# Attention and feed-forward kernel ordered by a planner: planned durations set anew, and the order rules of its stages chosen again

## The chip, the cores and the metric

The kernel runs on one core of a Trainium2 chip. The metric is the device time of one execution in microseconds; the median of several runs counts. The engines are called TensorE (PE), VectorE (DVE), ScalarE (ACT), GpSimd (POOL) and SyncE (SP).

## The reference

```python
x = A_x                                   # (1, 2048, 640) bf16
xn = _layernorm(x, axis=-1)
# A: 32 query heads of 20, one key and one value head for all of them
q = (xn @ wq).reshape(B, S, 32, 20).transpose(0, 2, 1, 3)
k = xn @ wk;  v = xn @ wv                 # (1, 2048, 20) each
p = softmax(einsum("bhqd,bkd->bhqk", q, k) * 20 ** -0.5)
a = einsum("bhqk,bkd->bhqd", p, v).transpose(0, 2, 1, 3).reshape(B, S, 640) @ wo
# B: 640 -> 1536 -> 640
h = relu(xn @ w1 + b1);  f = (h * h) @ w2 + b2
return x + a + f
```

## The kernel before

The work of attention is cut into 32 blocks: 4 chunks of 512 queries by 8 groups of 4 heads. A block has 16 key tiles of 128 keys, and each of them 4 score tiles (one per head) of 128 keys by 512 queries, so there are 2048 score tiles. TensorE makes a score tile into one PSUM bank; the four heads of a group lie on four row groups of the array, so that up to four score tiles run at once in one "visit" (the code's mode "R"). All other matmuls run in mode "C", four at once on four column groups. The planner charges `SWITCH` for a change of mode.

A score tile gets its exponential in one of two ways:

- ScalarE takes two neighbouring PSUM banks in one ACTIVATE (`make_act`, L1008; seldom one or three) and writes to the ring PT. When the four heads of a key tile are there, one group of four matmuls (`PV...`) adds its share of the values to the block's accumulator in PSUM.
- A *set* is a key tile whose four heads go to VectorE (`make_dqk`, `after_dqk`). VectorE makes a 16-bit integer from the score (L1197, `D1_...`), which read as bf16 is a straight-line approximation of a power of two. Three further terms are made from it by adding constants: *passes* `P1` to `P3`, on GpSimd (`int64_add`, four 16-bit elements at a time, L1217) or on VectorE (L1219). Each of the four terms would be a group of four value matmuls (`DPV...`). Two terms can be added up beforehand, which saves one group: by a DMA that accumulates and is issued from GpSimd (`AD...`, L1232) or by VectorE. The term buffers lie in the tensor tmore and, from the tenth on, in x_sb, which is no longer used by then.

Between them run the rest: layer norm at the start, the projections, the feed-forward part (`FFN...`, L738, L746), the output products, the normalisation of a block (`emit_norm`, through DRAM), and the tail with the last 512 rows.

The order of every engine's instructions is found when the kernel is built, by a list scheduler with planned durations: each `Op` has an engine, a duration and dependencies, and `ready()` adds a latency for each pair of engines (`LATS`) or one of its own. At each step the candidate that can start earliest is committed, with ties within `EPS` broken by priority. The chip then runs each engine's list in that order, with semaphores for the dependencies; the planned times themselves are not kept. For the adding transfers the planner knows the GpSimd time of an issue (`ADDUR`), the delay when the issue waits for a GpSimd pass (`ADPL`), the way to the start and to the landing (`ADLEAD`, `ADLAND`) and the distance between two transfers (`ADGAP`):

```python
if op.add:
    begun = max(s + ADLEAD, dma_free[0])
    dma_free[0] = begun + ADGAP
    op.lat = begun + ADLAND - op.fin
```

What the scheduler prefers is set by some thirty parameters with `DEFAULTS`; `RULES` overrides them for stages of 10 us (`STG`) of planned ScalarE time, stage 1 to 66 (`next_stage`, `par`). Those that the text below speaks of:

- `ADDM`: how many adding transfers a new set gets on average (0 to 2; `new_set`).
- `KEEP`, `KEEPX`, `KEEPM`: how many free PSUM banks must be left over before a VectorE score tile rides along, starts a visit of its own, or before another matmul unit starts; -1 in KEEPX or KEEPM means KEEP (`pool_banks`).
- `NOPEN`, `DVL`: how many sets may be open, and above what backlog of VectorE no tile is given to it.
- `PBIAS`: a pass goes to VectorE when GpSimd's backlog exceeds VectorE's by more than this many us.
- `MRG`, `M1`: whether two score steps share one visit. `P2`: VectorE tiles in a visit that follows a full one.
- `JIT`: how long before ScalarE runs dry a score step is issued.

GpSimd loads another instruction library (`LIB`) after its part of the layer norm and before its first pass.

## Time and profile before

| | |
|---|---|
| median of 3 runs (lowest to highest) | 670.59 us (669.18 to 670.64) |
| profiled execution, its own time | 671.5 us |
| its span, first to last instruction | 669.7 us |
| granted TensorE clock | 1.00 |
| busy PE, DVE, ACT, POOL | 661.3, 604.2, 651.9, 580.7 us |
| ScalarE's exponentials, VectorE's score tiles | 697, 652 |
| GpSimd's passes, VectorE's passes | 437, 52 |
| adding transfers | 133 |

In a row of the groups, the number behind the bar is busy time in us, then the mean duration of one in ns, then the idle time of the engine just before such instructions and what ended it. In a row of the timeline the first number is the start from the span's begin and the second the length, both in us; "x4" says how many instructions are merged. Durations of one engine can overlap: the next instruction starts before the last has ended. A row of a table by windows has start and end, the length, and then the busy time of PE, PEld, DVE, ACT and POOL, the granted clock, the share of the DMA engines and GB/s.

### The profile page before, as it was taken

The page shows a single profiled execution, that of the slowest core. Times are in us where ns is not written, and L with a number is a line of the kernel's source. Part 1 is how long each engine was busy: PE and PEld are TensorE (multiplying, and loading weights), DVE is VectorE, ACT ScalarE, POOL GpSimd, SP SyncE. Part 2 cuts the span into 40 slices and gives each one's busy share as a digit, 9 for nine tenths or more (in the row PEclk, how much of TensorE's full clock was granted, in tenths as well). Part 3 has the DMA queues.
Part 4 walks back from the last instruction along what each step waited for, and adds up shares of the span by engine and source line. Part 5 has one row for each costly group of instructions (what it writes and reads, how often), then busy time and mean ns, then how long its engine had stood idle before and what let it go on. Part 6 is the DMA issues. An engine that isn't in the chain of part 4 may idle for free.

```text
span 669.7 us, 22479 instructions
## 1 busy us (share of the span) xinstructions
PE 661.3 (99%) x9591; PEld 212.2 (32%) x9592; DVE 604.2 (90%) x1074; ACT 651.9 (97%) x720; POOL 580.7 (87%) x595
## 2 busy tenths in 40 slices
PE   9999999999999999999999999999999999999998
PEld 4532222333322222333333222233333332222354
DVE  8979999999999999998989999998998999999824
ACT  7999999999999999999999999999999999999995
POOL 1729899999999998999999999899999899989901
PEclk9999999999999999999999999999999999999999
DMA  8897776888777877697886876766678876987751
GB/s 289 229 249 158 166 158 131 174 165 170 168 153 140 168 137 135 135 195 156 159 176 121 167 147 123 148 124 140 127 165 167 170 151 131 173 164 150 162 128 52
DMA packets 55998, 105.80 MB, mean 158 GB/s; under 512 B 17106, under 2 KB 33250, under 8 KB 55834
## 3 DMA queue, kind: packets, MB, share of 16 engines
q0 software_dynamic: 19808, 72.36, 58.2%
q1 hardware_dynamic: 35514, 31.63, 16.6%
q8 instruction: 75, 1.23, 0.8%
q10 hardware_dynamic: 576, 0.38, 0.2%
q14 instruction: 25, 0.20, 0.1%
HBM read 22.81 MB, written 9.69 MB: 49 GB/s over the span
## 4 chain that ended last, share of the span: by engine, by line
PE 63%; ACT 19%; DMA 7%; POOL 5%; DVE 3%; issue 1%; SPq 1%; POOLq 0%
PE ps L424 62%; ACT PT L1008 19%; POOL x_sb L1217 3%; DMA tmore<-tmore 2%; POOL tmore L1217 2%; DMA x_sb<-tmore 2%; DVE tmore L1197 1%; DMA x_sb<-x_sb 1%; DMA x_sb<-in_A_x_dram 1%; DMA R<-drs 1%; PE ps L619 1%; POOL x_sb L1232 0%; DVE x_sb L1219 0%; SPq L719 0%; DVE big L746 0%
## 5 line engine op out<-in xcount | busy, mean ns | idle before, releaser
L1008 ACT ACTIVATE PT<-ps 128x1024 bf16<-128x1024 f32 x697 | 642.6, 1092 | 5.0 <-PE ps L424 4.6
L1197 DVE TENSOR_SCALAR tmore<-ps 128x512 uint16<-128x512 f32 x652 | 421.7, 683 | 36.5 <-PE ps L424 30.4
L1217 POOL INT64_ADD x_sb<-tmore x219 | 246.9, 1255 | 30.0 <-DVE tmore L1197 19.8
L424 PE MATMUL ps<-qT,kT 20*128 20x512 bf16 x2048 | 268.2, 384 | 1.7 <-ACT PT L1008 1.0
L1217 POOL INT64_ADD tmore<-tmore x218 | 248.5, 1273 | 22.3 <-DVE OR L1076 12.1
L424 PEld LDWEIGHTS ps<-qT,kT 20*128 20x128 bf16 x2048 | 67.4, 91 | 257.4 <-ACT PT L1008 227.4
L424 PE MATMUL ps<-PT,vx 128*32 128x512 bf16 x1396 | 134.2, 387 | 0.0
L424 PE MATMUL ps<-xnT,w_sb 128*32 128x512 bf16 x960 | 77.2, 383 | 0.2 <-DVE hT_tmp L738 0.2
L424 PE MATMUL ps<-w_sb,big 128*32 128x320 bf16 x1536 | 75.4, 301 | 0.0
L1232 POOL DMA_DIRECT2D tmore<-tmore x66 | 70.9, 1082 | 4.2 <-POOL tmore L1217 3.0
L1232 POOL DMA_DIRECT2D x_sb<-tmore x63 | 67.2, 1067 | 4.0 <-POOL x_sb L1217 2.2
L424 PE MATMUL ps<-tmore,vxs 128*32 128x512 bf16 x648 | 58.8, 383 | 0.6 <-POOL tmore L1217 0.6
L424 PE MATMUL ps<-x_sb,vxs 128*32 128x512 bf16 x636 | 57.5, 382 | 0.2 <-DMA x_sb<-x_sb 0.2
L424 PEld LDWEIGHTS ps<-PT,vx 128*32 128x32 bf16 x1396 | 34.2, 93 | 64.5 <-issue 59.9
L424 PE MATMUL ps<-tmore,vx 128*32 128x512 bf16 x468 | 44.5, 382 | 0.7 <-DMA tmore<-tmore 0.6
L424 PEld LDWEIGHTS ps<-w_sb,big 128*32 128x32 bf16 x1536 | 33.6, 96 | 27.3 <-issue 17.2
L738 DVE TENSOR_SCALAR hT_tmp<-ps,b1col 128x512 bf16<-128x512 f32 x48 | 35.6, 742 | 0.9 <-PE ps L424 0.5
L424 PE MATMUL ps<-xnT,wq_sb 128*32 128x512 bf16 (+2 forms) x480 | 33.8, 356 | 0.0
L424 PE MATMUL ps<-x_sb,vx 128*32 128x512 bf16 x324 | 31.8, 382 | 0.6 <-DMA x_sb<-tmore 0.6
L424 PE MATMUL ps<-wo_c,OC 128*32 128x320 bf16 x608 | 31.3, 301 | 0.0
L424 PEld LDWEIGHTS ps<-xnT,w_sb 128*32 128x32 bf16 x960 | 18.0, 94 | 25.9 <-issue 20.5
L826 DVE TENSOR_TENSOR out_sb<-ps,xr 128x320 bf16<-128x320 f32 x24 | 11.6, 484 | 13.2 <-PE ps L424 13.1
(93 smaller groups left out, 328.5 us busy)
## 6 DMA issues: line engine op xcount, KB each, us to landing
tmore<-tmore POOLq DMA_DIRECT2D x66, 512.0 KB, 5.5
x_sb<-tmore POOLq DMA_DIRECT2D x63, 512.0 KB, 5.4
w_sb<-in_B_w_dram SPq DMA_DIRECT2D x8, 480.0 KB, 11.2
big<-OR SPq DMA_DIRECT2D x71, 40.0 KB
big<-drs SPq DMA_DIRECT2D x71, 40.0 KB
xb<-in_A_x_dram SPq DMA_DIRECT2D x1, 2560.0 KB, 11.9
xb<-b2r POOLq DMA_DIRECT2D x1, 2560.0 KB, 20.3
xr<-xb SPq DMA_DIRECT2D x16, 160.0 KB, 4.4
```

The lines of the kernel that those rows point to most:

```text
L424: return lambda e: e.matmul(out_, l, r, start=start, stop=stop, tile_position=tp, skip_group_check=loose)
L619: return [(lambda e, dt=dt: e.transpose(out=psbf(bk)[:, dt * 128:(dt + 1) * 128], in_=xn_sb[:, st, dt:D:DT], identity=ident[:])) for dt in ...
L738: o = Op(f"RL{qc}_{f}", "DVE", 0.66, [lambda e: e.tensor_scalar(out=hT_tmp[:, k % 2, :], in0=ps[:, bk, :], scalar1=b1col[:, f:f + 1], scal ...
L826: o = Op(f"OE{n}", "DVE", 0.40, [lambda e: e.tensor_tensor(out=out_sb[:, slot, cs], in0=ps[:, bk, 0:HW], in1=xrow(st, cs), op=ALU.add)], [ ...
L1008: return Op(f"ACT{st_['j']}", "ACT", ACB + ACM * n, [lambda e: e.activation(out=PT[:, s0:s0 + n, :], in_=ps[:, b0:b0 + (n - 1) * db + 1:db ...
L1197: d1 = op(f"D1_{n}_{i}", "DVE", 0.60, lambda e: e.tensor_scalar(out=L[:, cs].bitcast(U16), in0=ps[:, bank, :], scalar1=XA, scalar2=XB, op0 ...
L1217: fn = lambda e, T=T, j=j: e.int64_add(out=T.bitcast(I64), in0=L.bitcast(I64), in1=TSTEP * j * 0x0001000100010001)
L1232: p = op(f"AD{a}_{n}", "POOL", ADDUR, lambda e, src=src, dst=dst: e.dma_start(dst, src, accum_op=ALU.add), dp + [ad_last.get(k)], dma=adse ...
```

## The change

No instruction is added or taken away in the code. Planned durations and latencies get other values, and the table RULES is replaced by another, for stages 1 to 66; what order comes out, and how many sets, passes and transfers, the planner decides from them.

```diff
-ADDUR = 0.875
-ADPL = 0.31
+ADDUR = 0.6
+ADPL = 0.62
...
-SWITCH = 0.105
-ACB, ACM = 0.0631, 0.4267
+SWITCH = 0.0995
+ACB, ACM = 0.05, 0.4267
...
-LATS = {("PE", "ACT"): 0.225, ("PE", "DVE"): 0.215, ("ACT", "PE"): 0.155, ...
+LATS = {("PE", "ACT"): 0.225, ("PE", "DVE"): 0.22, ("ACT", "PE"): 0.225, ...
...
-        lib_op = op("LIB", "POOL", 10.8, ...
+        lib_op = op("LIB", "POOL", 12.3, ...
...
-            return Op(f"PV{b}_{kt}", "PE", 0.222, parts, deps)
+            return Op(f"PV{b}_{kt}", "PE", 0.226, parts, deps)
...
-            return Op(f"DPV{b}_{kt}_{term}", "PE", 0.2205, parts, deps)
+            return Op(f"DPV{b}_{kt}_{term}", "PE", 0.226, parts, deps)
...
-                    r[0].lat = 0.425
+                    r[0].lat = 0.45
```

The steps of the other four-matmul units (KT, QC, Q1, FFN1 and the fill) go from 0.2205 to 0.224, those of the output products from 0.136 to 0.138. The pair of ScalarE is thereby planned at 0.05 + 2 x 0.4267 = 0.9034 us instead of 0.9165. Some of the rules, for stages 31, 45, 62 and 66:

```diff
-         31: {'PBIAS': 8, 'NOPEN': 3},
+         31: {'EVP': 0.3, 'PBIAS': 8, 'DGAP': 0.8, 'DLAST': 6, 'DRATE': 0.95, 'BEHIND': 0.12, 'IDLE': 0.3, 'EPS': 0.06, 'MRG': 1, 'M1T': 1.2, 'JIT': 0.8, 'PVA': 0.9, 'ND': 2, 'KEEP': 0, 'ADDM': 1.2, 'KEEPM': 2, 'KEEPX': -1, 'DVL': 99},
-         45: {'IDLE': 0.3, 'URG': 4, 'PVA': 0.8, 'PVD': 1.2, 'PP': 4, 'ND': 1, 'ADDM': 0, 'KEEPX': 2},
+         45: {'EVP': 0.3, 'PBIAS': 8, 'MPRIO': 0.3, 'DGAP': 0.8, 'DLAST': 6, 'DRATE': 0.95, 'BEHIND': 0.12, 'EPS': 0.06, 'MRG': 1, 'M1': 2, 'M1T': 1.2, 'ADDN': 0.6, 'ADP': 5, 'JIT': 0.8, 'R3': 9, 'PVA': 0.9, 'D1P': 0.3, 'ND': 2, 'KEEP': 0, 'ADDM': 1.2, 'KEEPM': 2, 'KEEPX': -1, 'DVL': 1.2, 'P2': 2},
-         62: {'EVP': 0.3, 'DGAP': 1.5, 'DRATE': 0.95, ..., 'NOPEN': 3, ..., 'KEEP': 2, 'ADPM': 2.4, 'KEEPM': 1, 'KEEPX': -1, 'DVL': 0.9, 'P2': 2},
+         62: {'EVP': 0.3, 'PBIAS': 8, ..., 'KEEP': 0, 'ADDM': 1.2, 'KEEPM': 2, 'KEEPX': -1, 'DVL': 99},
-         66: {'DGAP': 0.8, 'IDLE': 0.3, 'URG': 4, 'NOPEN': 1, 'MRG': 0, 'ADDN': 0.2, 'R3': 1, 'QKP': 0, 'ND': 1, 'KEEP': 0, 'KEEPM': 0, 'KEEPX': 2, 'DVL': 0.9}}
+         66: {'EVP': 0.3, 'PBIAS': 8, 'MPRIO': 0.5, 'DGAP': 0, 'DLAST': 6, 'DRATE': 0.95, 'BEHIND': 0.05, 'IDLE': 0.3, 'EPS': 0.03, 'MRG': 0, 'M1': 1, 'M1T': 1.2, 'ADDB': 1, 'JIT': 0.8, 'PVA': 0.9, 'SQP': 2, 'ND': 2, 'KEEP': 0, 'ADDM': 1.2, 'KEEPM': 2, 'KEEPX': -1, 'DVL': 99}}
```

The mean of a parameter over the 66 stages (with its default where a stage has no rule), before and after, for the parameters named above:

| | before | after | stages that differ |
|---|---|---|---|
| ADDM | 0.82 | 0.90 | 41 |
| KEEP | 0.82 | 0.55 | 44 |
| KEEPX | 1.98 | 0.79 | 42 |
| KEEPM | 0.58 | 1.06 | 40 |
| PBIAS | 5.5 | 6.0 | 24 |
| NOPEN | 2.2 | 2.2 | 23 |
| JIT | 0.86 | 0.83 | 40 |
| P2 | 0.26 | 0.44 | 27 |

## The prediction

> **What bounds the kernel now.** I read the page first: busy times and the chain that ended last, then the groups of instructions.

> ```profile
> PE 661.3 (99%) x9591; PEld 212.2 (32%) x9592; DVE 604.2 (90%) x1074; ACT 651.9 (97%) x720; POOL 580.7 (87%) x595
> PE 63%; ACT 19%; DMA 7%; POOL 5%; DVE 3%; issue 1%; SPq 1%; POOLq 0%
> L1008 ACT ACTIVATE PT<-ps 128x1024 bf16<-128x1024 f32 x697 | 642.6, 1092 | 5.0 <-PE ps L424 4.6
> L1197 DVE TENSOR_SCALAR tmore<-ps 128x512 uint16<-128x512 f32 x652 | 421.7, 683 | 36.5 <-PE ps L424 30.4
> ```

> ScalarE's exponentials (L1008) take 642.6 us and sat idle only 5.0. The other 652 score tiles go through VectorE (L1197): four to a set, so 163 sets. ScalarE has the other 2048 - 652 = 1396 tiles, two to a step in 697 steps. Second view, ScalarE's timeline: its start, an undisturbed stretch, and its end.

> ```profile
> 12.24 22.54 ACT L1008 ACTIVATE PT<-ps 128x1024 bf16<-128x1024 f32 x24
> 637.37 15.69 ACT L1008 ACTIVATE PT<-ps 128x1024 bf16<-128x1024 f32 x17
> 629.84 30.01 ACT L1008 ACTIVATE PT<-ps 128x1024 bf16<-128x1024 f32 x31
> ```

> The exponentials run from 12.24 to 629.84 + 30.01 = 659.85 us, and 12.24 + 642.6 + 5.0 + a tail of 669.7 - 659.85 = 9.85 make the span of 669.7. In the second row 17 steps take 15.69; less the last one's 1.09, a step starts every 0.91. So ScalarE gives time back only through fewer steps, not through better order: 697 x 0.91 = 634 of the 647.6 us from first to last is its floor, and 13 us at most are waits.

> TensorE is the other bound. Third view, its timeline in a quiet stretch:

> ```profile
> 485.23 0.39 PE L424 MATMUL ps<-qT,kT 20*128 20x512 bf16 x3
> 485.55 0.40 PE L424 MATMUL ps<-PT,vx 128*32 128x512 bf16 x4
> 485.78 0.39 PE L424 MATMUL ps<-x_sb,vxs 128*32 128x512 bf16 x4
> 486.10 0.39 PE L424 MATMUL ps<-qT,kT 20*128 20x512 bf16 x3
> ```

> From start to start: a group of four value matmuls is followed by the next group after 0.23 (485.55 to 485.78); a visit to the scores takes 0.32 to get in (485.78 to 486.10) and 0.32 to get out (485.23 to 485.55), 0.41 more than one group alone. There is no gap to squeeze in these rows; the changed order helps TensorE only with fewer groups or fewer visits. Fourth view, the stretch in which all engines work, and the waits of two of them:

> ```profile
> 45.00:637.00 592.00, 588.24 (x8208) 174.28 (x8200) 552.73 (x916) 588.38 (x641) 562.81 (x567) 1.00 0.77 155
> POOL x_sb L1217 <- DVE tmore L1197: 19.8, 1, 19.8
> POOL tmore L1217 <- DVE OR L1076: 12.1, 1, 12.1
> ```

> In these 592 us (busy PE, PEld, DVE, ACT, POOL) TensorE and ScalarE are idle under 4 us each, at a granted clock of 1.00; VectorE has 39 us left and GpSimd 29. GpSimd's two long waits lie outside: the library load before 45.6 us, and one after its last transfer. So what a new order can use is GpSimd's and VectorE's rest: more sets relieve ScalarE, more transfers that add two term buffers relieve TensorE.

> **GpSimd's transfer issues.** Here the planned numbers change most (0.875 to 0.6, and the delay behind a pass 0.31 to 0.62).

> ```profile
> 299.15 1.03 POOL L1217 INT64_ADD tmore<-tmore  x1
> 300.47 0.88 POOL L1232 DMA_DIRECT2D tmore<-tmore  x1 [0.30 <-POOL tmore L1217]
> 301.08 3.39 POOL L1217 INT64_ADD tmore<-tmore  x3
> 304.08 1.21 POOL L1232 DMA_DIRECT2D tmore<-tmore  x1
> 304.69 2.71 POOL L1217 INT64_ADD x_sb<-tmore  x2
> L1232 POOL DMA_DIRECT2D tmore<-tmore x66 | 70.9, 1082 | 4.2 <-POOL tmore L1217 3.0
> L1232 POOL DMA_DIRECT2D x_sb<-tmore x63 | 67.2, 1067 | 4.0 <-POOL x_sb L1217 2.2
> ```

> An issue lets the next pass start 0.61 after it (304.08 to 304.69); directly behind the pass that it needs there is 0.30 of waiting first (so 0.91). The old plan charged 0.875 and 1.185, the new 0.6 and 1.22. So the new plan is right for an issue with a pass in between, and charges 0.31 too much for a follower. The durations of 1.07 in the last two rows overlap the next instruction, and I do not take them as the price; they are the rival's.

> There are 133 issues (66 and 63 above and four between other buffers). If none follows its pass, the plan frees 133 x 0.275 = 36.6 us of GpSimd; if all do, it books 133 x 0.035 = 4.7 more. I take half: 66 x 0.275 - 67 x 0.035 = 15.8 us.

> **What the planner can buy with 15.8 us.** (1) *More adding transfers.* One replaces a group of four matmuls: 0.23 of TensorE for 0.61 of GpSimd. The share of them per set (ADDM) averages 0.82 over the 66 stages in the old rules and 0.90 in the new: 0.077 x 163 = 12 more. TensorE -12 x 0.23 = -2.8 us, GpSimd +7.3. Their landings are hidden behind other value groups as now. If that cover is gone a landing is paid in full, as at one place of the chain:

> ```profile
> 579.33 9.34 DMA tmore<-tmore
> 589.48 11.14 ACT L1008 ACTIVATE PT<-ps 128x1024 bf16<-128x1024 f32 x12 [0.64 <-PE ps L424]
> ```

> There the landing of 9.34 cost ScalarE 0.64 of idle time. (2) *More sets.* The new rules hold fewer PSUM banks back before a VectorE tile may start (KEEPX averages 1.98 before, 0.79 after; KEEP 0.82 and 0.55) and let GpSimd's backlog grow further (PBIAS 5.5 to 6.0). A set takes two steps off ScalarE, 2 x 0.91 = 1.8 us; on TensorE it takes off two visits (2 x 0.41, if its tiles ride along in other visits) and adds four groups, less the one that it replaces and 0.9 for transfers (2.1 x 0.23): -0.34. It costs VectorE 4 x 421.7/652 = 2.6 and GpSimd three passes of 1.01 and 0.9 x 0.61 = 3.6. What remains of the 15.8 after (1) is 8.5, so two sets: ScalarE -3.6, TensorE -0.7, VectorE +5.2 of its 39, GpSimd +7.2. No row gives the number of sets of the new order; the bounds are three fewer and six more, since six at 3.6 = 21.6 with (1) already take GpSimd's whole 29. Two is my choice within it.

> (3) *The library load*, planned at 10.8, now 12.3:

> ```profile
> 32.64 0.87 POOL L508 TENSOR_SCALAR big<-x_sb,mv,rstd 128x640 bf16<-128x640 bf16 x1
> 45.61 4.08 POOL L1217 INT64_ADD tmore<-tmore  x4 [12.09 <-DVE OR L1076]
> 45.61 2.06 POOL tmore L1217 x2
> 47.71 15.53 PE ps L424 x195
> 48.47 25.97 ACT L1008 ACTIVATE PT<-ps 128x1024 bf16<-128x1024 f32 x28 [0.48 <-PE ps L424]
> ```

> 33.51 to 45.61 is 12.1. The third and fourth rows are pieces of the chain; they show TensorE held by those late passes, and ScalarE lost 0.48. A plan that knows it puts other work there: -0.5 on both (bounds 0 and -0.5).

> (4) *The rest of the numbers.* Value groups go from 0.2205 or 0.222 to 0.226, projections to 0.224, a mode switch from 0.105 to 0.0995, a ScalarE pair from 0.9165 to 0.9034, ScalarE to TensorE from 0.155 to 0.225. Against rows of 0.23, 0.41 and 0.91 these are small, and they charge no time themselves; they alter which instruction the search puts next. A better match should save part of ScalarE's 5.0 us of idle time and of its 13 us over the floor, but a new order can also add waits: between +3 and -5, and I take -1.0, a fifth of the visible idle time.

> Sum on ScalarE's path: -3.6 - 0.5 - 1.0 = -5.1. On TensorE's: -2.8 - 0.7 - 0.5 - 1.0 = -5.0. Neither bound hides the other, so I take the smaller, **-5.0 us**. The start (12.24) and the tail (9.85) stay but for what the rules of the first and last stages shuffle, at most 1 us either way. Against the profiled execution: 671.5 (span 669.7 and 1.8 around it) - 5.0 = 666.5. That execution is 0.9 above the median of 670.59; on the median, **665.6**.

> What moves past what, with the passes that VectorE makes:

> ```profile
> L1219 DVE TENSOR_SCALAR tmore<-tmore 128x2048 uint16<-128x2048 uint16 x27 | 21.0, 786 | 0.2 <-PE ps L424 0.2
> L1219 DVE TENSOR_SCALAR x_sb<-tmore 128x2048 uint16<-128x2048 uint16 x25 | 20.8, 838 | 0.7 <-PE ps L424 0.7
> ```

> The rules set the order of every engine's list, SP's and GpSimd's included. A transfer issue that is put behind a further pass lands 1.01 later, and the group that reads it waits in TensorE's list in order, with the next score visit queued behind it, and ScalarE behind that. With PBIAS raised, some of VectorE's 52 passes go to GpSimd, and each holds what is queued behind it there for 1.01.

> **Rivals.** *A. Larger gain.* If all 36.6 us are freed and go into transfers, that is 60 x 0.23 = 13.8 us of TensorE, and ScalarE would need seven sets to follow, one above the bound. I cap it at -12.6: 658. Against it: ADDM rises by 0.077 only.

> *B. No gain.* That the durations were set to recorded ones would not hold in full: the follower's 0.62 against a recorded 0.30. If the rules still let half of the issues follow, plan and chip have the idle 0.3 as before, no set is added, and the saved library wait is what is left: 670, the same. For it: the charge for a follower hardly changes (1.185 to 1.22). The bound of "same" here is 0.3%, 2 us, about what a measurement of this kernel can tell from no change.

> *C. Slower: GpSimd falls behind its own plan.* The price of an issue on the chip may be more than 0.6, because VectorE's operations hold it up.

> ```profile
> L1232 POOL DMA_DIRECT2D tmore<-tmore x66: 843/1004/1733, 61.9 to 635.7; - x66
> L1232 POOL DMA_DIRECT2D x_sb<-tmore x63: 844/930/1931, 55.9 to 623.5; - x63
> L1217 POOL INT64_ADD x_sb<-tmore x219: 1027/1197/1993, 51.1 to 658.9; - x110
> L1217 POOL INT64_ADD tmore<-tmore x218: 1027/1312/2002, 45.6 to 634.1; - x109
> ```

> Issues reach 1.7 and 1.9 us (minimum, median, maximum in ns). With 145 issues and 219 + 218 + 6 = 443 passes at 1.01, GpSimd's load is 447 + 145c. It fills the 592 us at c = 1.0; the old plan's 0.875 to 1.185 covered that, the new 0.6 does not. At c = 1.07, the mean of the rows, it is 602: 10 us too many. Term buffers then come free late, VectorE waits for them, its PSUM banks are held, and TensorE and ScalarE stop. Half of the 10 us would be taken up by the idle time that GpSimd has; I give +5.4, 676. Against it: the 0.61 from start to start in both examples, which says that much of 1.07 is overlap. [...]

> *D. Slower for lack of cushion.* A planned pair of 0.9034 lies below the 0.91 of the rows; the old 0.9165 lay above, and 697 x 0.013 = 9 us of planned slack vanish. Scores are then placed a little too early and TensorE stands in order before a bank that ScalarE has not left. If a third of the 9 us returns as waits and no set is added: +3, 674.

> **How the numbers follow.** Forecast 0.45 (its own range 661 to 668.5), A 0.11, B 0.14, C 0.22, D 0.08. Faster by over 0.3%: 0.45 + 0.11 = 0.56; within: 0.14; slower: 0.22 + 0.08 = 0.30. The range of 658 to 676 takes in A's and C's prices and leaves out about half of C and of A, under 2 in 10.

> **What would show it.** Right: L1197 at 660 or so instead of 652 and L1008 near 693; some 145 rows of L1232; GpSimd's busy time nearer 592 in the same stretch; no 0.48 of ScalarE before 48 us. Step (1) is wrong if L1232 stays at 133; step (2) if L1197 does not rise. C would show as waits of L1197 for L1217 or for landings, and as ScalarE idle time above 10 us; D as the step count unchanged with more waits. The prediction is wrong altogether if the number of sets falls.

## The result and the profile after

The changed kernel took 698.88 us (median of 6 runs, 693.16 to 709.51) against 670.51 for the kernel before. The ratio is 1.0394, with a 95% interval of 1.0341 to 1.0447; here and below, ratios leave out the runs that lie more than 1.5% above the quickest of the same kernel, in which the clock was lowest. The forecast was 665.6 in a range of 658 to 676. The runs after spread widely, and the mean clock that TensorE was granted goes with their times; the spans and mean granted clocks were 691.4 (0.988) in the quickest and 707.7 (0.959) in the profiled one, which is the slowest of the six.

The page of the changed kernel, its totals and groups (line numbers are four higher than before):

```profile
PE 691.1 (98%) x9519; PEld 215.5 (30%) x9519; DVE 606.1 (86%) x1043; ACT 662.4 (94%) x722; POOL 610.4 (86%) x622
PEclk9599999999699999999996888999999999999999
L1012 ACT ACTIVATE PT<-ps 128x1024 bf16<-128x1024 f32 (+1 forms) x699 | 653.2, 1090 | 33.3 <-PE ps L428 31.6
L1201 DVE TENSOR_SCALAR tmore<-ps 128x512 uint16<-128x512 f32 x644 | 416.3, 681 | 61.4 <-PE ps L428 55.4
L1221 POOL INT64_ADD tmore<-tmore x230 | 287.8, 1502 | 37.4 <-DVE tmore L1201 29.4
L1221 POOL INT64_ADD x_sb<-tmore x225 | 280.6, 1513 | 15.6 <-PE ps L428 9.8
L1236 POOL DMA_DIRECT2D x_sb<-tmore x68 | 88.3, 1299 | 2.2 <-DVE OC L1106 1.3
L1236 POOL DMA_DIRECT2D tmore<-tmore x72 | 83.7, 1181 | 1.9 <-POOL tmore L1221 1.9
L1223 DVE TENSOR_SCALAR tmore<-tmore 128x2048 uint16<-128x2048 uint16 x13 | 13.5, 1037 | 0.0
L1223 DVE TENSOR_SCALAR x_sb<-tmore 128x2048 uint16<-128x2048 uint16 x15 | 18.9, 1262 | 0.0
```

Three things are to be seen. ScalarE has 699 steps instead of 697, and its idle time has gone from 5.0 us to 33.3, nearly all of it ended by TensorE. The sets have fallen from 163 to 161 (644 tiles). And GpSimd has more to do: 455 passes instead of 437, since VectorE makes only 28 of them instead of 52 (and takes 1037 and 1262 ns for one on average, instead of 786 and 838), and 142 adding transfers instead of 133 (two more lie between other buffers). At the 1.01 of a pass and 0.6 of an issue, that is 18 x 1.01 + 9 x 0.6 = 23.6 us more load on GpSimd.

Then the clock (the row PEclk above). Windows of the changed kernel, in the columns of the prediction's window row: the same 592 us, one stretch of half clock, and the stretch behind it.

```profile
45.00:637.00 592.00, 581.53 (x7656) 166.37 (x7648) 530.63 (x844) 567.28 (x611) 554.44 (x556) 0.97 0.76 153
182.60:196.25 13.65, 13.65 (x124) 3.11 (x124) 6.09 (x10) 8.19 (x8) 9.77 (x10) 0.50 0.63 132
196.30:210.00 13.70, 13.70 (x198) 4.09 (x198) 12.78 (x22) 13.70 (x16) 12.37 (x15) 1.00 0.73 147
```

At half clock TensorE issues 124 matmuls where it issues 198 at full clock, and ScalarE makes 8 steps instead of 16. There are four such stretches in this execution, of 17.1, 13.65, 17.1 and 10.2 us, 58 in all (the first begins at 15.35 us, ahead of the first row); the kernel before has none from 0 to 637 us (its clock there was 1.00). What stands in front of them is in TensorE's timeline; in brackets is how long it stood still and for what:

```profile
182.43 0.49 PE L428 MATMUL ps<-x_sb,vx 128*32 128x512 bf16 x4 [1.80 <-DMA x_sb<-tmore]
182.85 0.61 PE L428 MATMUL ps<-qT,kT 20*128 20x512 bf16 x4
183.40 0.62 PE L428 MATMUL ps<-tmore,vxs 128*32 128x512 bf16 x4
376.18 0.40 PE L428 MATMUL ps<-tmore,vxs 128*32 128x512 bf16 x4 [1.46 <-POOL tmore L1221]
415.97 0.40 PE L428 MATMUL ps<-tmore,vxs 128*32 128x512 bf16 x4 [0.37 <-POOL tmore L1221]
417.90 0.45 PE L428 MATMUL ps<-tmore,vxs 128*32 128x512 bf16 x4 [0.88 <-POOL tmore L1221]
```

TensorE's value groups wait for GpSimd's passes, or for transfers that GpSimd issued late, and soon after the stop every matmul takes longer (groups of four go from 0.40 to 0.62).

### The profile page after: what moved, and what is told of

Same layout as the page of the kernel before. It is cut to its first block, busy times and chain, and to the rows that moved or that the text cites. A ratio compares the mean times of both kernels' runs of the same rounds, so it can differ in the third digit from the quotient of the medians.

```text
span 707.7 us, 22341 instructions
## 1 busy us (share of the span) xinstructions
PE 691.1 (98%) x9519; PEld 215.5 (30%) x9519; DVE 606.1 (86%) x1043; ACT 662.4 (94%) x722; POOL 610.4 (86%) x622
## 3 DMA queue, kind: packets, MB, share of 16 engines
q1 hardware_dynamic: 35514, 31.63, 15.5%
q8 instruction: 74, 1.21, 0.7%
## 5 line engine op out<-in xcount | busy, mean ns | idle before, releaser
L1012 ACT ACTIVATE PT<-ps 128x1024 bf16<-128x1024 f32 (+1 forms) x699 | 653.2, 1090 | 33.3 <-PE ps L428 31.6
L1201 DVE TENSOR_SCALAR tmore<-ps 128x512 uint16<-128x512 f32 x644 | 416.3, 681 | 61.4 <-PE ps L428 55.4
L1221 POOL INT64_ADD tmore<-tmore x230 | 287.8, 1502 | 37.4 <-DVE tmore L1201 29.4
L1221 POOL INT64_ADD x_sb<-tmore x225 | 280.6, 1513 | 15.6 <-PE ps L428 9.8
L428 PE MATMUL ps<-qT,kT 20*128 20x512 bf16 x2048 | 283.9, 395 | 2.7 <-DVE tmore L1201 0.7
L428 PEld LDWEIGHTS ps<-qT,kT 20*128 20x128 bf16 x2048 | 71.0, 91 | 275.2 <-ACT PT L1012 203.1
L428 PE MATMUL ps<-PT,vx 128*32 128x512 bf16 x1404 | 138.6, 399 | 0.2 <-DVE OR L1080 0.2
L1236 POOL DMA_DIRECT2D x_sb<-tmore x68 | 88.3, 1299 | 2.2 <-DVE OC L1106 1.3
L1236 POOL DMA_DIRECT2D tmore<-tmore x72 | 83.7, 1181 | 1.9 <-POOL tmore L1221 1.9
L428 PE MATMUL ps<-x_sb,vx 128*32 128x512 bf16 x320 | 32.4, 395 | 1.8 <-DMA x_sb<-tmore 1.8
L750 DVE TENSOR_TENSOR big<-hT_tmp 128x512 bf16<-128x512 bf16 x48 | 33.5, 700 | 0.2
L428 PEld LDWEIGHTS ps<-xnT,w_sb 128*32 128x32 bf16 x960 | 18.5, 95 | 24.3 <-issue 19.5
```

The source lines that it names most:

```text
L428: return lambda e: e.matmul(out_, l, r, start=start, stop=stop, tile_position=tp, skip_group_check=loose)
L750: q = op(f"SQ{qc}_{f}", "DVE", 0.34, lambda e: e.tensor_tensor(out=h2T[:, f, :], in0=hT_tmp[:, k % 2, :], in1=hT_tmp[:, k % 2, :], op=ALU. ...
L1012: return Op(f"ACT{st_['j']}", "ACT", ACB + ACM * n, [lambda e: e.activation(out=PT[:, s0:s0 + n, :], in_=ps[:, b0:b0 + (n - 1) * db + 1:db ...
L1201: d1 = op(f"D1_{n}_{i}", "DVE", 0.60, lambda e: e.tensor_scalar(out=L[:, cs].bitcast(U16), in0=ps[:, bank, :], scalar1=XA, scalar2=XB, op0 ...
L1221: fn = lambda e, T=T, j=j: e.int64_add(out=T.bitcast(I64), in0=L.bitcast(I64), in1=TSTEP * j * 0x0001000100010001)
L1236: p = op(f"AD{a}_{n}", "POOL", ADDUR, lambda e, src=src, dst=dst: e.dma_start(dst, src, accum_op=ALU.add), dp + [ad_last.get(k)], dma=adse ...
```

## The experiments

All runs are compared with the kernel before on the same chip.

**Filling TensorE's stops.** The changed order with groups of matmuls on zeros put in front of eight operations that waited longest, so that TensorE does not stand still there.

```diff
+MID = {'DPV7_14_1': 7, 'DPV11_11_3': 4, 'DPV16_11_3': 6, 'DPV18_12_2': 2, 'DPV18_12_3': 4, 'DPV29_11_3': 3}
+FIRST = {'QK2': 2, 'QK3': 2}
...
+for o in order_all:
+    n, fn = (MID[o.name], fill_parts) if o.name in MID else (FIRST.get(o.name, 0), warm_parts)
+    for _ in range(n):
+        filled.append(Op("fill", "PE", 0.224, fn()))
+    filled.append(o)
```

> The changed order, with 30 zero matmul groups of 0.22 us put in front of the eight TensorE instructions at which the profile shows TensorE standing still (the six longest waits on passes and landings, and the second and third score visit). No other engine's list is touched. Theory 'clock': the stops themselves cost only their own length, and the half-clock stretches behind them (58 us of the profiled run) cost 0.37 us each us; with the groups in place the granted clock is 0.99 to 1.00 and the time 685 to 689. Theory 'late GpSimd alone': the clock follows the waits but costs little; the time stays at 693 to 700.

It took 691.13 us (4 runs, 687.97 to 702.25), 1.0299 of the kernel before (1.026 to 1.0338). Its profiled run:

```profile
core 0: 686.2 us, clock 1.000
L1012 ACT ACTIVATE PT<-ps 128x1024 bf16<-128x1024 f32 (+1 forms) x699 | 650.4, 1090 | 13.9 <-PE ps L428 12.0
175.23 1.68 PE L428 MATMUL ps<-kT,zeros 128*32 128x512 bf16 x28
```

The third row is the filling in front of the group that the landing held up. With no half clock the span is 686.2 (687.6 in another run at clock 1.0), so the new order loses 16.5 us (686.2 - 669.7) without any loss of clock. The rest comes with the clock: 58 us at half clock go with (707.7 - 686.2) = 21.5 us, 0.37 per us. The two windows above say the same: 124 matmuls in place of 198 are 37% fewer. What was expected of theory 'clock' holds for the runs at full clock (687.97 us, and 689.39 just over the 689). The other two, at clocks of 0.993 and 0.978, took spans of 691.1 and 700.5: the filling did not prevent every such stretch. Against a filled order at full clock, the quickest run of the changed kernel (691.4) lost 5 us to the clock.

**Taking load off GpSimd.** The passes cover 480 of their 512 64-bit columns (the terms' last columns are left as they were); a second dose leaves 448.

```diff
-... e.int64_add(out=T.bitcast(I64), in0=L.bitcast(I64), ...)
+... w=(480 if k >= NT else 512): e.int64_add(out=T.bitcast(I64)[:, 0:w], in0=L.bitcast(I64)[:, 0:w], ...)
```

> The changed order; every GpSimd pass from the fourth set on works on 480 of 512 elements (the last 6% of a term's columns are left out), so that each takes about 0.06 us less: 27 us over 440 passes, as much as the old plan charged too much for the issues. Theory 'lost cushion': GpSimd keeps up with its plan, the stops of over 1 us are gone, the clock stays at 1.00 after the start and the time is 668 to 676. Theory 'VectorE is late': 688 to 698.

> The changed order, passes on 448 of 512 elements (12% left out), about 0.1 us less each: twice the dose. Theory 'cushion': the first 24 us bought 17 at full clock, and then something else holds the order; the second dose buys little, 664 to 669. Rival 'GpSimd is the bound throughout': it buys as much again, 650 to 656.

> The order before, with every GpSimd pass from the fourth set on working on 480 of 512 elements (6% of a term's columns left out). Theory 'lost cushion': GpSimd is not what holds this order, it gains little: 666 to 670. Rival 'shorter passes help any order': 650 to 660, as the changed order gained 20 and more.

On the changed order: 670.8 us (10 runs), 1.0017 (0.9995 to 1.0038); its profiled run, with a span of 675.4 us, has one stretch of half clock near the start, while others had spans of 668.1 to 669.3 at clock 1.0. With 448 columns: 669.41 (10 runs), 0.9998 (0.9974 to 1.0023). On the old order with 480: 668.08 (10 runs), 0.9985 (0.9958 to 1.0013). The changed order with 480 columns, GpSimd's passes and ScalarE:

```profile
L1221 POOL INT64_ADD tmore<-tmore x230: 976/1282/2367, 52.1 to 657.8; - x115
L1012 ACT ACTIVATE PT<-ps 128x1024 bf16<-128x1024 f32 (+1 forms) x699 | 645.7, 1161 | 8.7 <-PE ps L428 8.4
```

and the same ScalarE group with 448 columns, then of the old order with 480:

```profile
L1012 ACT ACTIVATE PT<-ps 128x1024 bf16<-128x1024 f32 (+1 forms) x699 | 643.8, 1190 | 2.7 <-PE ps L428 2.6
```

```profile
L1008 ACT ACTIVATE PT<-ps 128x1024 bf16<-128x1024 f32 x697 | 641.3, 1108 | 2.6 <-PE ps L424 2.3
```

The shortest pass falls from 1028 to 976 ns; over the 445 shortened passes (the first ten are whole) that is 23 us, about as much as the new order had added (23.6), and with it all of the loss is gone. By the ratios the next 24 us buy only 1.3 us, and the same cut on the old order only 1.0 (both within their intervals): ScalarE then has 2.7 and 2.6 us of idle time left and is the bound. The first and the last of the three expectations are met, and the second dose bought as little as its theory said (669.41 us, just over its 669). So GpSimd's load has an edge somewhere in these 24 us: the old order lies on the good side of it, the new one beyond. TensorE's waits for passes into `tmore` show it, in the changed kernel and with 480 columns (us in all, number, longest):

```profile
PE ps L428 <- POOL tmore L1221: 5.5, 7, 1.5
```

```profile
PE ps L428 <- POOL tmore L1221: 0.6, 2, 0.4
```

**VectorE's collisions, or VectorE's time.** One run shortens VectorE's score tiles, which read PSUM (468 of 512 columns; the rest of the terms is not written). The other shortens those operations of VectorE that have two inputs in SBUF or work on 16-bit data from SBUF to SBUF: the squares, the normalising products of half of the query chunks, and its own passes (they cover 32, 32 and 128 columns, and the rest is left out).

```diff
-... e.tensor_scalar(out=L[:, cs].bitcast(U16), in0=ps[:, bank, :], ...
+... e.tensor_scalar(out=L[:, c2].bitcast(U16), in0=ps[:, bank, 0:w2], ...
```

> The changed order; VectorE's score tiles from the sixth set on work on 468 of 512 columns (the rest of the tile is left out), 0.045 us less each, 28 us over the kernel: the same dose as for GpSimd, on the other engine. Theory 'lost cushion on GpSimd': little help, 686 to 698. Theory 'VectorE is late': 668 to 676.

```diff
-... e.tensor_tensor(out=h2T[:, f, :], in0=hT_tmp[:, k % 2, :], in1=hT_tmp[:, k % 2, :], op=ALU.mult)
+... e.tensor_tensor(out=h2T[:, f, 0:32], in0=hT_tmp[:, k % 2, 0:32], in1=hT_tmp[:, k % 2, 0:32], op=ALU.mult)
...
-... e.tensor_scalar(out=T.bitcast(U16), in0=L.bitcast(U16), scalar1=TSTEP * j, ...
+... w=(128 if k >= NT else 2048): e.tensor_scalar(out=T.bitcast(U16)[:, 0:w], in0=L.bitcast(U16)[:, 0:w], ...
```

> The changed order; the operations of VectorE that have two inputs in SBUF or run on 16-bit data in SBUF are cut short: the squares (L750) and the normalising products of the last two query chunks to 32 columns, its 28 passes to 128 (the rest of them is left out). That takes about 33 us of VectorE, and nearly all of its collisions with GpSimd's passes. Theory 'collisions': the time falls to 668 to 676 and the excess of a pass behind such an operation vanishes. Theory 'GpSimd has too much work whatever VectorE does': 686 to 698. If it falls here and not with the shorter score tiles, collisions and not VectorE's load are what counts.

Shorter score tiles gave 705.32 us (4 runs, 696.59 to 715.64), spans 694.8 to 713.8 at clocks of 0.983 to 0.955: no help. Shorter operations of the second kind gave 683.1 (4 runs), 1.0116 (1.0089 to 1.0142), with spans of 675.5 and 676.4 at full clock, 10 us under the 686.2 of the filled order. These two runs took 677.37 and 678.22 us, a little over the 668 to 676 that theory 'collisions' expected.

```profile
L1201 DVE TENSOR_SCALAR tmore<-ps 128x468 uint16<-128x468 f32 (+1 forms) x644 | 391.5, 638 | 69.9 <-PE ps L428 66.0
```

The first run took 25 us of busy time off VectorE's score tiles (391.5 for 416.3) and gained nothing, so VectorE's time is not the bound. The second points at operations of VectorE whose length varies. In the trace of the changed kernel all 644 score tiles take 0.619 to 0.693 us, 630 of them beside an instruction of GpSimd; the squares take 0.407 to 1.246 and VectorE's own passes 0.681 to 1.931. The squares show it from run to run. Minimum, median and maximum in ns for the kernel before, after, after with 480 columns, and for the short squares:

```profile
L746 DVE TENSOR_TENSOR big<-hT_tmp x48: 361/417/1516, 49.1 to 613.6; 128x512 bf16<-128x512 bf16 x48
```

```profile
L750 DVE TENSOR_TENSOR big<-hT_tmp x48: 407/667/1246, 54.8 to 656.6; 128x512 bf16<-128x512 bf16 x48
```

```profile
L750 DVE TENSOR_TENSOR big<-hT_tmp x48: 366/421/1467, 54.5 to 624.4; 128x512 bf16<-128x512 bf16 x48
```

```profile
L750 DVE TENSOR_TENSOR big<-hT_tmp x48: 157/366/1683, 55.0 to 635.1; 128x32 bf16<-128x32 bf16 x48
```

The same square of the same shape takes 0.36 us at best and 0.42 in the middle in the kernel before, 0.67 in the changed one, and 0.42 again once GpSimd's passes are 5% shorter. Even a square of 32 columns, 0.157 at best, has a median of 0.366, 0.21 more than at best.

GpSimd's issues get longer as well. An issue of the changed kernel, the pass behind it, and VectorE at the same time:

```profile
299.72 1.55 POOL L1236 DMA_DIRECT2D tmore<-tmore  x1
301.17 1.19 POOL L1221 INT64_ADD tmore<-tmore  x1
299.72 1.26 DVE L1223 TENSOR_SCALAR tmore<-tmore 128x2048 uint16<-128x2048 uint16 x1
```

Here the next pass starts 1.45 us after the issue and not 0.61, and VectorE's pass, which takes 0.68 at best in this trace, takes 1.26. Counted over the whole trace from 45 us on, 128 issues have the next GpSimd instruction right behind them without idle time. 28 of these hold GpSimd for over 0.8 us, 15.5 us more in all than 0.605 each, and all 28 lie beside a square, a normalising product or a pass of VectorE; of the other 100, 28 do. In the kernel before it is 20 of 97, with 8.9 us. The planner keeps GpSimd's passes apart from these operations of VectorE (their `lock`), and the code even makes each pass wait for the last one planned before it (L1448); but the adding transfers' issues have no `lock`, so the plan lets them collide. With VectorE's operations cut short there are still 29 such issues, with 11.7 us. So the collisions did not vanish, as the expectation asked, and how the 10 us of that run divide between GpSimd and VectorE stays open.

In the rows above both sides get longer where they meet, 1.45 us for 0.61 and 1.26 for 0.68; which of the two holds up the other, and by what, no run here shows.

**The converse on the old order.** If the new order fails because GpSimd has lost its slack, the old one must fail when its slack is filled. A memset that nothing reads follows each adding transfer:

```diff
+pad = sb("pad", [128, 208], F32)
...
+late_ = Op("slow", "POOL", 0.27, [lambda e: e.memset(pad[:], 0.0)], [late_])
+slowed.append(late_)
```

> The order before, with one GpSimd memset of 208 floats per partition on an unused tensor behind each of its 133 adding transfers. It gives GpSimd about as much extra work as the old plan charged too much for an issue (0.2 to 0.3 us each, 27 to 36 us in all; the profile shows the exact length). Theory 'lost cushion': without the cushion the old order falls behind its plan like the new one: 680 to 700, with stops of TensorE over 1 us and a clock that may drop below 1.00. Rival 'the new rules are worse by themselves': the old order takes it nearly unharmed, 669 to 674.

It took 693.84 us (4 runs), 1.034 (1.0297 to 1.0383), with spans of 688.2 and 690.0 at clocks of 1.0 and 0.998. GpSimd's timeline, and the groups of the memsets and of ScalarE:

```profile
316.57 0.88 POOL L1233 DMA_DIRECT2D x_sb<-tmore  x1 [0.30 <-POOL x_sb L1218]
317.13 0.60 POOL L1564 MEMSET pad<- 128x208 f32 x1
317.38 1.36 POOL L1218 INT64_ADD x_sb<-tmore  x1
L1564 POOL MEMSET pad<- 128x208 f32 x133 | 120.0, 902 | 0.0
L1009 ACT ACTIVATE PT<-ps 128x1024 bf16<-128x1024 f32 x697 | 650.8, 1047 | 17.8 <-PE ps L425 15.8
```

A memset holds GpSimd for 0.25 us from start to start (317.13 to 317.38), 133 x 0.25 = 33 us in all. That is less than the 36.6 by which 0.875 overcharges 133 issues of 0.6, and yet the order with the old charge, given the time that it had been charged, falls 18.5 us behind (688.2 - 669.7), with 17.8 us of idle time on ScalarE instead of 5.0. So the overcharge was not lying idle: it covered what the plan does not know of. Nor do the memsets take time from GpSimd alone. The squares of this run, with a median of 0.61 us where it was 0.42:

```profile
L747 DVE TENSOR_TENSOR big<-hT_tmp x48: 356/614/1960, 49.0 to 633.5; 128x512 bf16<-128x512 bf16 x48
```

How much of the loss comes by way of VectorE is not separated.

**Landings.** The transfers move half of their bytes (half of each sum is missing):

```diff
-... e.dma_start(dst, src, accum_op=ALU.add)
+... e.dma_start(dst[:, 0:1024], src[:, 0:1024], accum_op=ALU.add)
```

> The changed order; each adding transfer moves half of the columns (the other half of the sum is left out), so that it lands sooner and loads the DMA engines half as much, while GpSimd issues as many. Theory 'landings': the longest stop of TensorE, 1.8 us behind a landing, says that the transfers are late; the time falls to 670 to 680. Theory 'GpSimd is late before it issues': little help, 686 to 700, unless the issue itself gets shorter with the transfer, which the profile would show.

706.21 us (4 runs), 1.0423 (1.0381 to 1.0465). The transfers of the changed kernel and of this one:

```profile
tmore<-tmore POOLq DMA_DIRECT2D x72, 512.0 KB, 5.4
```

```profile
tmore<-tmore POOLq DMA_DIRECT2D x72, 256.0 KB, 4.0
```

Landings 1.4 us earlier help nothing; the median is even a little over the expected 700, at clocks of 0.945 to 0.978. TensorE's waits, first for landings in `x_sb` in the changed kernel and with half the bytes, then for passes with half the bytes:

```profile
PE ps L428 <- DMA x_sb<-tmore: 1.8, 1, 1.8
```

```profile
PE ps L428 <- DMA x_sb<-tmore: 0.4, 1, 0.4
PE ps L428 <- POOL tmore L1221: 6.2, 8, 1.5
```

The wait for landings shrinks and that for passes does not (it was 5.5). What is late is the passes, not the way of the transfers.

**Half of the change at a time.** The new durations with the old rules, and the old durations with the new rules. Each gives a third and a fourth order, since the planner plans anew.

```diff
-ADDUR = 0.875
+ADDUR = 0.6
... (all durations as after; RULES as before)
```

> One half of the change alone: the new durations with the rules of before. The planner makes another order of it: by its own count it ends at 687.7 us (before 659.9, changed 656.9), with 153 sets, 440 passes on GpSimd and 124 transfers. Theory 'a plan without slack on GpSimd is not kept': here GpSimd has 440 x 1.015 + 124 x 0.57 + 33 = 550 us of work in 688, 80%, so the chip keeps the plan within about 12 us: 693 to 702. Rival 'the new durations are wrong in themselves': the chip is 30 us or more behind as with the changed kernel, 717 or more.

```diff
-RULES = ... (before)
+RULES = ... (after; all durations as before)
```

> The other half alone: the new rules with the durations of before. The planner's own count is 704.0 us, with 149 sets, 411 passes on GpSimd and 134 transfers. Theory 'slack on GpSimd': 411 x 1.015 + 134 x 0.57 + 33 = 527 us in 704, 75%; the chip keeps the plan within about 12 us: 708 to 718. Rival 'the new rules make orders that the chip cannot keep': 30 us or more behind, 734 or more. Either way each half is slower than both kernels, since the rules were chosen for their own durations.

New durations alone: 709.26 us (3 runs), 1.0596 (1.051 to 1.0682), with 153 sets, planned to end at 687.7; at full clock its span was 703.5, 15.8 behind plan. New rules alone: 716.68 us (3 runs), 1.0713 (1.0674 to 1.0752), with 149 sets, planned to end at 704.0; its profiled span of 714.5 is 10.5 behind plan, about 6 of it in one stretch of half clock. ScalarE's idle time (the groups of each run):

```profile
L1008 ACT ACTIVATE PT<-ps 128x1024 bf16<-128x1024 f32 (+1 forms) x713 | 662.3, 1124 | 25.0 <-PE ps L424 24.2
```

```profile
L1012 ACT ACTIVATE PT<-ps 128x1024 bf16<-128x1024 f32 (+1 forms) x719 | 668.3, 1121 | 26.4 <-PE ps L428 25.9
```

The new rules alone are in the range that the slack theory gave (708 to 718); the new durations alone are in neither of their two ranges (693 to 702, or 717 and more), since they lag by 15.8 and not 12. Neither half is a kernel that anyone would want: the rules were chosen for their own durations, and most of the loss of both lies in the plan itself. The lag behind the plan is the useful number. With the old durations it is 9.8 for the old rules (669.7 against a planned 659.9) and at most 10.5 for the new ones; with the new durations it is 15.8, and 29 for the changed kernel (686.2 at full clock against a planned 656.9). By estimate some 5 us of lag come with the new durations by themselves, because they let the plan end earlier (worked out under the fourth step in the next section); less these, the new durations alone lag about as much as the old ones. So the large lag shows only where the new durations and the new rules come together. Which duration does it can't be isolated by setting one at a time, because every setting yields another order.

## Why the prediction was wrong

The step that failed is **what the planner can buy with 15.8 us**, together with the price of an issue on which it rests. It took the overcharge of an issue, and the 29 us that GpSimd had idle, as time to spend. At the median the price was right. In the changed kernel's GpSimd timeline the next pass still starts 0.61 after an issue:

```profile
163.29 2.09 POOL L1236 DMA_DIRECT2D x_sb<-tmore  x1
163.90 2.58 POOL L1221 INT64_ADD x_sb<-tmore  x1
```

But on average it was not. From start to start, the 97 issues of the kernel before that have the next instruction right behind them took 0.71 us, and the 128 of the changed kernel 0.73, because of the long ones shown above. Over 133 issues that tenth of a us is some 14 us, so of the time that the prediction counted as free a large part was in use already. The rest did not lie idle either: the converse run filled the overcharge and lost 18.5 us, and taking 23 us off GpSimd's passes in the changed order brought all of the loss back. (The half of the issues that the prediction let follow their pass was off too, the other way: the waits of the kernel before show 17.)

**(1) More transfers, (2) more sets.** Transfers rose by 9, not 12, and TensorE has fewer matmuls (9519 for 9591). Sets fell by two instead of rising by two, which the prediction named as the sign that it is wrong altogether. The planner spent its freed time on a third thing, which the prediction mentioned under "what moves past what" but left out of the sum: VectorE has 24 passes fewer, GpSimd 18 more, and six fewer are needed in all for two fewer sets. Of 23.6 us of added load 18.2 are these passes.

**(3) The library load.** In the profiled run the first pass starts later than before (45.61), as TensorE was at half clock from 15.3 to 32.4 us and VectorE's first tiles came late.

```profile
52.28 2.06 POOL L1221 INT64_ADD tmore<-tmore  x2 [11.80 <-DVE tmore L1201]
36.65 23.94 ACT L1012 ACTIVATE PT<-ps 128x1024 bf16<-128x1024 f32 x26 [1.33 <-PE ps L428]
```

The second row is ScalarE in the filled run at full clock: it goes on without a stop from 36.65 to 60.59, so the 0.48 of idle time at 48 us is gone, as forecast.

**(4) The rest of the numbers,** put at -1.0 between +3 and -5. With GpSimd relieved until ScalarE is the bound in both, the new order took a span of 667.7 (448 columns, clock 0.999) and the old 665.5 (480 columns, clock 1.0), though planned 3.0 us shorter (656.9 for 659.9). Two more steps at 0.91 are 1.8 of these 2.2 us. So no gain of the new order is to be seen even with GpSimd out of the way: its better plan came, as far as these runs tell, out of shorter planned numbers, such as ScalarE's pair of 0.9034 against 0.91. That is where rival D starts, and it accounts for some 5 us of the lag (10.8 behind plan against 5.6). D's waits did not come, though: ScalarE's idle time in that run is 2.7 us. The plan is too short by that much, and the kernel does not get longer by it.

**Rival C** had the direction, the place and the sign in the profile right: GpSimd behind its own plan, and ScalarE's idle time above 10 us (13.9 in the filled run at full clock). Of its mechanism, issues that VectorE's operations hold up, the trace of the changed kernel shows this much: all 28 long issues counted above (over 0.8 us) lie beside a square, a normalising product or a pass of VectorE, and only 28 of the other 100 do. That VectorE is what holds them was the author's reading. Its sizes were not right: at the measured 0.73 an issue, GpSimd's load is 455 x 1.01 + 142 x 0.73 = 563 us and does not fill the 592, so by C's own reckoning nothing would be lost. That its sum came out slower rests on the 1.07, which is not the price, and is in that part luck. The load does not have to fill the 592 us before it costs something, since the order of every list is fixed and a pass that is late holds TensorE at that place (seven waits for passes into `tmore`, 5.5 us in all, the longest 1.5). At full clock the loss is 16.5 us and not 5.4. Shortening VectorE's operations took about 10 of it away, shortening GpSimd's passes all of it; the two cannot be added up.

**What nobody had on the list** is the clock. Between 5 and 21 us of the loss, varying from run to run, go with stretches of half clock, which in the profiled run stand behind stops of TensorE that last under 2 us (1.80, 1.46, and 0.37 with 0.88, in front of three of the four).

## What to carry to other kernels

A planned duration above the recorded one may be slack on which the order depends: before lowering it, lengthen the real operation on the chip by the difference, in the old order; if that costs time, the charge was not idle. Take the price of an operation from start to start, as the mean over all its occurrences and not from two rows, and look at what runs beside the long ones. Idle time of an engine in a profile is no stock that can be booked: add load in the form of dummy work, or take some away, and see on which side of the edge the kernel stands. Compare plan and chip by the lag of each order behind its own plan, not by the planned ends, and look at the granted clock whenever runs of one kernel spread.

## What the runs showed of the hardware

```profile
179.19:182.60 3.41, 1.61 (x20) 0.42 (x19) 3.41 (x6) 1.92 (x2) 3.41 (x6) 1.00 0.98 204
373.75:377.16 3.41, 1.95 (x31) 0.52 (x23) 1.79 (x4) 1.93 (x3) 3.41 (x5) 1.00 0.80 154
414.71:418.12 3.41, 2.17 (x30) 0.60 (x22) 2.98 (x6) 2.88 (x4) 3.41 (x6) 1.00 0.77 155
271.31:274.72 3.41, 2.54 (x33) 0.64 (x29) 2.05 (x4) 2.51 (x3) 3.41 (x5) 1.00 0.88 178
267.90:271.31 3.41, 3.00 (x41) 0.85 (x38) 3.41 (x7) 3.41 (x5) 3.41 (x6) 1.00 0.89 177
```

TensorE was idle for 1.80, 1.46 and 1.24 us of the first three (3.41 less its busy time) and for 0.87 and 0.41 of the last two. The third and the last two hold nearly the same thing: two stops 1.93 us apart, of 0.37 and 0.88 at 416 to 418 us, and of 0.41 and 0.87 at 270.5 to 272.4. The first pair lies within one step and stands before 10.24 us of half clock; the second is divided between two steps, and no drop follows it. Whether it is the grid that makes this difference no run here shows, nor what sets the spread from run to run. The idle time of the step before does not separate the drops from the rest: before the first drop (11.93 to 15.34) it was 1.01 us, another step of this trace (117.75 to 121.16) had 1.28 without a drop, and in the run with the new rules alone a step with 0.52 stands right before a drop of 17.07 us:

```profile
653.27:656.68 3.41, 2.89 (x26) 0.92 (x24) 3.38 (x6) 3.41 (x5) 2.05 (x3) 1.00 0.80 157
656.68:673.75 17.07, 16.77 (x105) 3.21 (x102) 11.60 (x20) 12.47 (x13) 12.60 (x14) 0.50 0.69 130
```

Once down in the changed kernel, the clock stayed at half for 10.24 to 17.07 us, three to five steps, with TensorE busy all through (13.65 of 13.65 us in the stretch shown, 17.06 of 17.06 twice and 10.23 of 10.23 in the others). In the run with the shorter score tiles one stretch of half clock, from 354.45 us on, lasted a single step of 3.41 us.
